# Stores of two blocks at a time, and q and k in four pieces, in an attention and expert kernel

## The chip, the cores and the metric

The kernel runs on one core of a Trainium2 chip. The core has a matrix engine (TensorE, PE in the profile; its weight loads are PEld), three engines for elementwise work (VectorE = DVE, ScalarE = ACT, GpSimd = POOL), a sequencer that here only issues transfers (SyncE = SP, "SPq"), and 16 DMA engines. The metric is the device time of one execution in microseconds (us), as a median of several runs. A profile shows one further execution.

## The reference

Attention with a sliding window of 128 and a linear bias, over 8 batches, 8 heads, 576 positions and 64 elements a head; its result x (4608 tokens of 512) goes through eight experts, all of them applied to all tokens and weighted by a matrix P that eight rounds of row and column normalisation make from the gate's logits.

```python
def _attn_ref(q, k, v):
    scores = scale * np.matmul(q, k.transpose(0, 1, 3, 2))
    rel = pos[:, None] - pos[None, :]
    bias = slopes[:, None, None] * (-np.abs(rel).astype(np.float32))[None, :, :]
    mask = (rel >= 0) & (rel < window)
    scores = np.where(mask, scores + bias[None], -1000000000.0)
    ...
    return np.matmul(attn, v).astype(np.float32)

def _moe_ref(x, w_gate, w1, w2):
    logits = x @ w_gate
    logits = logits - logits.max()
    P = np.exp(logits)
    for _ in range(8):
        P /= P.sum(1, keepdims=True) + 1e-09
        P /= P.sum(0, keepdims=True) + 1e-09
        P *= N / E
    out = np.zeros((N, D), dtype=np.float32)
    for e in range(E):
        h = np.maximum(x @ w1[e], 0.0)
        ye = h @ w2[e]
        out += P[:, e:e + 1] * ye
    return out.astype(np.float32)
```

## The kernel before

The program is written in the order in which each engine runs it (`tc.manual_schedule()`): an engine's queue is the order of the calls, and waits are put in where a tile's data or its buffer isn't there yet. SP issues nearly all transfers, so a transfer that must wait holds up those behind it.

**Attention stage (to about 284 us).** The main loop (L689) goes through 80 steps (b, kb, u): batch b, block kb of its five key blocks (four of 128 positions and a last one of 64), half u of the heads; at = 2 kb + u is the step within a batch. A step does the next step's scores (PE, L403) and exponentials (ACT, L426), its masks (DVE, L438), and its own values (L449: PE into a tile psN, then a reciprocal and a product on DVE into the tile xsb). When both halves of a block are there, `turn_x` (L496) turns it into xT: on PE for batches 0 to 2 and 7, with a transposing DMA (L519) for batches 3 to 6. It also puts the block on the list `kept`, from which `keep_x` stores it to the DRAM tensor xd (L494), three blocks later. Batch 0 occupies about 10 to 34 us; from batch 3 on (107 us) a batch takes 32 to 37 us.

**Filler.** PE's free time in these steps is filled with experts 0 and 1 (class Filler, L170), whose results need no P. A unit is four blocks of x and one expert: eight pieces of the first layer (`l1`, L109: four matmuls into psh, then a ReLU on ACT, L127) and four of the second (`l2`, L131: eight matmuls into psy, L137). Each l2 ends in `keep` (L545): DVE casts psy to a tile yo (L555), and a store to the DRAM tensor ysp is put on the list `stores`. `store(2)` ahead of each cast issues what is older than the last two (L541). The tag yo has YO = 6 tiles of 128 x 512 f16, so the cast of the sixth result after it waits until a result's store has landed. psy, psh, psN and some other PSUM tiles share the tag pmm, of four. Only the first four blocks of expert 0 go another way (y_first, L551). A batch has about eight l2.

**q and k.** Batch b + 2 is loaded at step (b, 3) for b = 1 to 5: `load_qk(b + 2)` (L766), one transfer of 1 MB each for q and k into two tiles (L271). They are cast to f16 by `cast_qk`, q on DVE (L287) and k on ACT (L289), two heads at a time: pieces 0 and 1 at steps (b, 8) and (b, 9), pieces 2 and 3 at (b + 1, 0) and (b + 1, 1). From batch 3 on `turn_qk` (at = 1, two transposing DMAs, L301), then `load_tail` (L260, "t") and `turn_tail` (at = 5, tT, L320) follow on SP. `load_v` (L374) follows every block.

**Afterwards.** The gate's logits are turned into P on DVE (L814 to L852) while the filler goes on, to about 326 us; then the main expert loop (L1104, experts 2 to 7, with a fast matrix product of seven products) reads xd two blocks at a time into xtok (L880), scales them (L888), turns them with transposing DMAs (L898) and adds the stored results of experts 0 and 1 (`load_y`, L1021). xs, xtok and s3 take buffers of the tag yo there, and t16 (the tails) takes one of the tag xsb (XSB = 12).

Of the kernel before, what the change touches and what calls it, by code (L numbers as in the profile page):

```python
# [9 lines left out]
FP16 = mybir.dt.float16  # L10
FP32 = mybir.dt.float32
# [3 lines left out]
def kernel(  # L15
# [10 lines left out]
    nc = tc.nc  # L26
# [137 lines left out]
            yield 0, a  # L164

    L1_US, L2_US = 0.87, 1.74
    XPE, YO, XSB = 3, 6, 12
    CAST_AT = ((0, 1, 2, 3), (1, 2, 3, 4))

    class Filler:  # L170
# [57 lines left out]
    sps = first_pool.enter_context(tc.tile_pool(name="sps", bufs=1, space=bass.MemoryType.PSUM))  # L228
    if True:
        mask = asb.tile([P, H, 2 * P], FP16, name="mask")  # L230
        rel = per.tile([P, HD], FP16, name="rel", tag="yo", bufs=YO)[:, 0 : 2 * P]

        def make_mask(ys):
            for y in ys:
# [27 lines left out]
                )  # L262
            tails[b] = t32

        def load_qk(b, parts=1):
            q32 = per.tile([P, H, RI * Dh], FP32, name=f"q32_{b}", tag="a8", bufs=8)
            k32 = per.tile([P, H, RI * Dh], FP32, name=f"k32_{b}", tag="a8", bufs=8)
            w = H // parts
            for n in range(parts):
                for t, src in ((q32, q), (k32, k)):  # L270
                    nc.sync.dma_start(  # L271
                        out=t[:, n * w : n * w + w],
                        in_=src[b, n * w : n * w + w, 0:SM, :].rearrange("h (p i) d -> p h (i d)", i=RI),
                    )
            raw[b] = (q32, k32)

        def cast_qk(b, j, which=(1, 0), pool=False):

# [36 lines left out]
                )  # L315

        def turn_tail(b):
            t16 = asb.tile([P, HD], FP16, name=f"t16_{b}", tag="xsb", bufs=XSB)
            nc.gpsimd.tensor_copy(out=t16, in_=tails.pop(b).rearrange("p h d -> p (h d)"))
            nc.sync.dma_start(out=QKT[b][2], in_=t16, transpose=True)  # L320

# [123 lines left out]
            )  # L445

        xsbs: dict = {}

        def values(b, kb, u):  # L449

            nk, _ = sizes(kb)
            if u == 0:
                xsbs[b, kb] = asb.tile([P, H, Dh], FP16, name=f"xsb_{b}_{kb}", tag="xsb", bufs=XSB)
            psN = aps.tile([P, GT], FP32, name=f"psN_{b}_{kb}_{u}", tag="pmm", bufs=4)
            if b == 0:
                spin(psN, 3)
            psN = psN[:, 0 : 4 * Dh + 4].rearrange("p (h d) -> p h d", h=4)
            ops = []
            for y in range(2):
                for hb in range(2):  # L460
                    hh = 2 * y + hb
                    if kb > 0:
                        ops.append((hh, pts[b, kb - 1, u][:, 2 * hb + y, P : P + nk], vs[b, kb - 1][:, 4 * u + hh, 0 : Dh + 1]))
                    ops.append((hh, pts[b, kb, u][0:nk, 2 * hb + y, 0:nk], vs[b, kb][0:nk, 4 * u + hh, 0 : Dh + 1]))
            if kb == NKB - 1:
                ops = ops[0::2] + ops[1::2]
            for i, (hh, lhsT, rhs) in enumerate(ops):
                nc.tensor.matmul(  # L468
                    out=psN[0:nk, hh, :],
                    lhsT=lhsT,  # L470
                    rhs=rhs,
                    start=(i == 0),
                    stop=(i == len(ops) - 1),
                )
            if kb > 0:
                pts.pop((b, kb - 1, u))
            rden = asb.tile([P, 4], FP32, name=f"rden_{b}_{kb}_{u}", tag="rden", bufs=2)
            nc.vector.reciprocal(out=rden[0:nk, :], in_=psN[0:nk, :, Dh])
            nc.vector.tensor_tensor(
                out=xsbs[b, kb][0:nk, 4 * u : 4 * u + 4, :],  # L480
                in0=psN[0:nk, :, 0:Dh],
                in1=rden[0:nk, :].unsqueeze(2).to_broadcast([nk, 4, Dh]),
                op=ALU.mult,
            )
# [5 lines left out]

        def keep_x(left=0):
            while len(kept) > left:
                blk, lo, nk, xsb = kept.pop(0)
                nc.sync.dma_start(out=xd[blk, lo : lo + nk, :], in_=xsb[0:nk].rearrange("p h d -> p (h d)"))  # L494

        def turn_x(b, kb):  # L496
            nk, _ = sizes(kb)
            blk = 4 * b + kb if kb < NKB - 1 else 4 * B + b // 2
            lo = 0 if kb < NKB - 1 else TL * (b % 2)
            xT, at = x_of(blk)  # L500
            to = xT[:, at, :, lo : lo + nk]
            xsb = xsbs.pop((b, kb))
            if by_pe(b):
                ps = aps.tile([P, NDT, P], FP16, name=f"psX_{b}_{kb}", tag="pmm", bufs=4)
                for j in range(NDT):
                    nc.tensor.matmul(
                        out=ps[:, j, 0:nk],
                        lhsT=xsb[0:nk, 2 * j : 2 * j + 2, :],
                        rhs=ident[0:nk, 0:nk],
                        is_transpose=True,  # L510
                        start=(j == 0),
                        stop=(j == NDT - 1),
                    )
                if b == 0:
                    nc.scalar.copy(out=to, in_=ps[:, :, 0:nk])
                else:
                    nc.vector.tensor_copy(out=to, in_=ps[:, :, 0:nk])  # L517
            else:
                nc.sync.dma_start(out=to, in_=xsb[0:nk].rearrange("p h d -> p (h d)"), transpose=True)  # L519
            kept.append((blk, lo, nk, xsb))  # L520
            keep_x(3)

        def gates(b0, b1):
            ps = aps.tile([P, b1 - b0, E], FP32, name=f"psG_{b0}", tag="pmm", bufs=4)
# [13 lines left out]
        def store(left=0):  # L538
            while len(stores) > left:
                e, blk, yo = stores.pop(0)  # L540
                nc.sync.dma_start(out=ysp[e, blk], in_=yo)  # L541

        first_y: list = []

        def keep(e, blk, ps):  # L545
            if blk < RI and e == 0:
                if not first_y:
                    first_y.append(per.tile([P, RI, HD], FP16, name="y_first", tag="a8", bufs=8))
                nc.vector.tensor_copy(out=first_y[0][:, blk, :], in_=ps)
                if blk == RI - 1:  # L550
                    nc.sync.dma_start(out=ysp[0, 0:RI].rearrange("m p d -> p m d"), in_=first_y[0])  # L551
                return
            store(2)
            yo = per.tile([P, HD], FP16, name=f"yo_{e}_{blk}", tag="yo", bufs=YO)
            nc.vector.tensor_copy(out=yo, in_=ps)  # L555
            stores.append((e, blk, yo))

        order = [(0, 0, 2), (0, 2, 2)]
        for b0 in range(RI, NBLK, 4):
# [92 lines left out]
        load_first()  # L652
        spin_alone(20)
        make_mask(range(4))
        load_qk(1, 2)
        load_v(NKB)
        load_tail(1)
        cast_v(0)
# [30 lines left out]
        for n, (b, kb, u) in enumerate(steps):  # L689
# [67 lines left out]
            if (b, at) == (1, 2):  # L757
                filler.hold = False
            if (b, at) == (0, 9):
                load_qk(2, 2)  # L760
            if (b, at) == (0, 7):
                homes(1)
            if (b, at) == (1, 3):
                homes(2)
            if 1 <= b < B - 2 and at == 3:
                load_qk(b + 2)  # L766
            if XPE <= b + 1 < B - 1 and at >= 8:
                cast_qk(b + 2, at - 8)
            if XPE <= b + 1 < B:
# [112 lines left out]
        def scale_x(n):  # L882
            if n >= N:
                return
            g, e = units[n]
            for m in range(2):
                blk = 2 * g + m
                nc.scalar.mul(out=xs[2 * (n % 2) + m], in_=xtok[m], mul=P_sb[:, blk, e : e + 1])  # L888
            if e == E - 1 and n + 1 < N:
                if g == groups[0]:  # L890
                    xtok[:] = [per.tile([P, HD], FP16, name=f"xtok_{i}", tag="yo", bufs=YO) for i in range(2)]
                load_x(units[n + 1][0])

        def turn_xs(n):
# [19 lines left out]
        def quads_w1(e):  # L914
# [5 lines left out]
            elif e == E - 1:  # L920
                t = per.tile([P, 2, 2, HF], FP16, name=f"s_{e}", tag="xT", bufs=4)
                q.update(s1=t[:, 0], s2=t[:, 1])
                q["s3"] = [per.tile([P, HF], FP16, name=f"s3_{k}", tag="yo", bufs=YO) for k in range(2)]
            else:
                q.update((f"s{i}", aux[:, i].rearrange("p f n -> p (f n)").rearrange("p (k f) -> p k f", k=2)) for i in (1, 2, 3))
            q["s4"] = q["a21"]
            SL[e] = q

            def one(to, a, b, op):
                if isinstance(q[to], list):  # L930
                    for k in range(2):
                        nc.vector.tensor_tensor(out=q[to][k], in0=q[a][:, k], in1=q[b][:, k], op=op)
                else:
                    nc.vector.tensor_tensor(out=q[to], in0=q[a], in1=q[b], op=op)

            one("s1", "a21", "a22", ALU.add)
            one("s3", "a11", "a21", ALU.subtract)
# [30 lines left out]
        def part(n, ps, w, x, start=False):  # L968

            q = SL[units[n][1]][w]  # L970
            q = q if isinstance(q, list) else [q[:, k] for k in range(2)]
            for j in range(NF2):
                for k in range(2):
                    nc.tensor.matmul(  # L974
                        out=ps[:, j, :],
                        lhsT=q[k][:, P * j : P * j + P],
                        rhs=xset[n % 2][:, x, P * k : P * k + P],
                        start=(start and j == 0 and k == 0),
                        stop=(k == 1),
# [119 lines left out]
        s5 = s5y[:, 0].rearrange("p (f t) -> p f t", f=NF2)  # L1099
        y = s5y[:, 1].bitcast(FP16).rearrange("p (m d) -> p m d", m=2)  # L1100
        turn_xs(1)
        xs[:] = [per.tile([P, HD], FP16, name=f"xs_{i}", tag="yo", bufs=YO) for i in range(2)] * 2
        late: tuple = ()
        for n in range(N):  # L1104
            g = units[n - 1][0]
# [103 lines left out]
```

## Time and profile before

| what | us |
|---|---|
| median of 3 runs (lowest, highest) | 1025.33 (1023.34, 1028.51) |
| the profiled execution | 1025.63 |
| its span in the profile | 1023.9 |
| PE busy / DVE / ACT / POOL | 1000.3 / 749.5 / 722.2 / 78.8 |
| ysp<-yo stores: 68 of 128 KB, issue to landing, median | 3.3 |
| xd<-xsb stores: 32 of 128 KB and 8 of 64 KB | 3.1 and 5.1 |
| q and k loads of 1 MB: 5 each | 7.8 and 10.1 |
| q and k pieces of 256 KB at the start: 4 each | 5.2 and 4.8 |
| s5y<-ysp loads of 256 KB: 36 | 3.0 |

The granted TensorE clock is 1.00 throughout. In a timeline a row has the start in us, the duration, the engine, the line, the operation and its tiles (out<-in), and in brackets the idle time ahead of it and what ended it. SPq rows are issues: their duration is the time for which SP was held. A row of waits has the total, the number and the longest.

### The profile page before, as it was taken

To read this page: it belongs to the slowest core of one execution; us is meant where nothing else is said; L and a number is where in the kernel's file an instruction comes from. 1 tells how busy PE (TensorE), PEld (TensorE's weight loads), DVE (VectorE), ACT (ScalarE), POOL (GpSimd) and SP (SyncE) were. 2 spreads that over 40 slices of the span, in tenths; PEclk is the share of its full clock that TensorE was granted. 3 is DMA by queue.
4 is the path that set the end of the run, shared out by engine and by line. 5 is a ranking of instruction groups with operands and counts; after the bars stand their busy time and mean duration, and the time that the engine had idled before them with its cause. 6 is when DMAs were issued, how large, how long until landed. Compare 5 with 4: busy or idle time off the path is not lost.

```text
span 1023.9 us, 27787 instructions
## 1 busy us (share of the span) xinstructions
PE 1000.3 (98%) x11487; PEld 801.6 (78%) x11487; DVE 749.5 (73%) x1594; ACT 722.2 (71%) x1240; POOL 78.8 (8%) x143
## 2 busy tenths in 40 slices
PE   7999999999999999999999999999999999999998
PEld 5645444444544698999999999999999999999997
DVE  5735665556578588877877877877887887787787
ACT  7646555555433457888888888888888888888885
POOL 1212033306110000000000000000000000000000
PEclk9999999999999999999999999999999999999999
DMA  9996689889999233343334334324334434333461
GB/s 244 219 271 170 143 221 220 191 196 180 221 192 177 69 72 80 71 81 94 74 64 100 76 66 94 73 64 94 77 65 98 81 71 81 86 82 65 98 115 47
DMA packets 264431, 122.46 MB, mean 120 GB/s; under 512 B 201968, under 2 KB 255728, under 8 KB 264304
## 3 DMA queue, kind: packets, MB, share of 16 engines
q1 hardware_dynamic: 249568, 102.68, 44.2%
q0 software_dynamic: 14304, 17.84, 10.5%
q8 instruction: 90, 1.47, 0.6%
q14 instruction: 37, 0.30, 0.1%
q10 hardware_dynamic: 432, 0.16, 0.1%
HBM read 78.30 MB, written 23.59 MB: 100 GB/s over the span
## 4 chain that ended last, share of the span: by engine, by line
PE 74%; DVE 3%; DMA 1%; ACT 1%; issue 0%; DVEq 0%; ACTq 0%; SPq 0%
PE psM L1011 30%; PE psB L974 13%; PE psA L974 9%; PE psC L974 9%; PE psy L137 5%; PE psh L115 5%; PE psh L953 2%; DVE acc L1055 1%; PE psN L468 1%; DMA acc<-xd 0%; DVE hs L1141 0%; PE psS L412 0%; DVE hs L991 0%; DVE hs L992 0%; DMA s5y<-ysp 0%
## 5 line engine op out<-in xcount | busy, mean ns | idle before, releaser
L1011 PEld LDWEIGHTS <-hs 128*128 128x128 f16 x2996 | 271.7, 98 | 22.4
L1011 PE MATMUL psM<-w2l,hs 128*128 128x256 f16 x1440 | 186.6, 273 | 0.0
L974 PEld LDWEIGHTS <-w1l 128*128 128x128 f16 x2720 | 173.2, 98 | 8.9 <-issue 3.0
L127 ACT ACTIVATE hT<-psh 128x512 f16<-128x512 f32 (+1 forms) x144 | 83.3, 586 | 100.9 <-PE psh L115 100.2
L987 ACT ACTIVATE hs<-hs 128x512 f16<-128x512 f16 x204 | 125.0, 630 | 34.3 <-DVE hs L1141 34.1
L1141 DVE TENSOR_TENSOR hs<-psB,s5y 128x512 f16<-128x512 f32 x102 | 70.4, 690 | 103.7 <-ACT xs L888 95.9
L115 PE MATMUL psh<-xT,w1t 128*128 128x512 f16 (+1 forms) x608 | 139.8, 368 | 3.2 <-DVE xT L517 2.4
L974 PEld LDWEIGHTS <-s 128*128 128x128 f16 x2040 | 135.3, 98 | 5.8
L888 ACT ACTIVATE xs<-xtok,L_sb 128x512 f16<-128x512 f16 x204 | 136.0, 720 | 0.6 <-DMA xset<-xs 0.6
L137 PE MATMUL psy<-w2t,hT 128*128 128x512 f16 x576 | 134.3, 379 | 0.0
L1011 PE MATMUL psM<-more,hs 128*128 128x256 f16 x864 | 129.0, 273 | 0.0
L974 PE MATMUL psA<-xset,w1l 128*128 128x128 f16 x1360 | 103.7, 219 | 0.0
L974 PE MATMUL psB<-xset,s 128*128 128x128 f16 x1360 | 103.7, 219 | 0.0
L137 PEld LDWEIGHTS <-hT 128*128 128x128 f16 x576 | 53.5, 98 | 60.9 <-issue 1.5
L555 DVE CAST yo<-psy 128x512 f16<-128x512 f32 x68 | 46.8, 690 | 72.1 <-PE psy L137 57.8
L115 PEld LDWEIGHTS <-w1t 128*128 128x128 f16 x608 | 54.7, 98 | 54.7 <-issue 7.0
L991 DVE TENSOR_TENSOR hs<-hs 128x1024 f16<-128x1024 f16 x107 | 74.0, 691 | 23.5 <-ACT hs L987 16.8
L430 ACT ACTIVATE pt<-psS 128x1024 f16<-128x1024 f32 (+2 forms) x80 | 67.7, 851 | 29.2 <-PE psS L412 22.7
L1135 ACT COPY psC<-psB 128x512 f32<-128x512 f32 x102 | 58.1, 570 | 36.5 <-PE psB L974 36.5
L1130 ACT COPY s5y<-psC 128x512 f32<-128x512 f32 x102 | 59.8, 586 | 25.5 <-PE psC L974 25.5
L443 DVE TENSOR_TENSOR pt<-pt,mask 128x1024 f16<-128x1024 f16 (+2 forms) x80 | 51.8, 647 | 32.8 <-ACT pt L430 32.7
L1055 DVE TENSOR_TENSOR acc<-acc,psM 128x256 f32<-128x256 f32 (+1 forms) x162 | 74.1, 503 | 2.1
(121 smaller groups left out, 1410.1 us busy)
## 6 DMA issues: line engine op xcount, KB each, us to landing
s5y<-ysp SPq DMA_DIRECT2D x36, 256.0 KB, 3.0
ysp<-yo SPq DMA_DIRECT2D x68, 128.0 KB, 3.3
v<-in_v_dram SPq DMA_DIRECT2D x32, 256.0 KB, 4.4
out_dram<-acc SPq DMA_DIRECT2D x31, 256.0 KB, 2.5
q<-in_q_dram SPq DMA_DIRECT2D x5, 1024.0 KB, 7.8
k<-in_k_dram SPq DMA_DIRECT2D x5, 1024.0 KB, 10.1
xtok<-xd SPq DMA_DIRECT2D x34, 128.0 KB, 2.3
w2t<-in_moe_w_dram POOLq DMA_DIRECT2D x4, 1024.0 KB, 10.9
```

Of the source, the lines that this page charges most:

```text
L115: nc.tensor.matmul(out=ps[:, 0:nt], lhsT=w1ts[e][:, dt, P * ft : P * ft + P], rhs=xT[:, at : at + nb, dt, :], start=(dt == 0), stop=(dt == ...
L127: nc.scalar.activation(out=st["hT"][:, ft, 0:nt], in_=ps[:, 0:nt], func=AF.Relu)
L137: nc.tensor.matmul(out=ps, lhsT=st["hT"][:, ft, P * ms : P * ms + P], rhs=w2ts[e][:, ft, :], start=(ft == 0), stop=(ft == NFT - 1),)
L430: nc.scalar.activation(out=pt[0:nk, :, 0 : nk + nn], in_=ps[0:nk, :, :, 0 : nk + nn].rearrange("p a y n -> p (a y) n"), func=AF.Exp, scale ...
L888: nc.scalar.mul(out=xs[2 * (n % 2) + m], in_=xtok[m], mul=P_sb[:, blk, e : e + 1])
L974: nc.tensor.matmul(out=ps[:, j, :], lhsT=q[k][:, P * j : P * j + P], rhs=xset[n % 2][:, x, P * k : P * k + P], start=(start and j == 0 and ...
L987: nc.scalar.activation(out=h[n][:, slot], in_=src, func=AF.Relu)
L991: nc.vector.tensor_tensor(out=t[:, 4:6], in0=t[:, 0:2], in1=t[:, 2:4], op=ALU.add)
L1011: nc.tensor.matmul(out=Ms[bk][:, half, :], lhsT=h[n][:, LEFT[m], f, :], rhs=W2L[e][RIGHT[m]][:, f, :], start=(e == 2 and f == 0 and half = ...
L1055: nc.vector.tensor_tensor(out=a, in0=a, in1=p2, op=op)
L1130: nc.scalar.copy(out=s5, in_=pc)
L1141: nc.vector.tensor_tensor(out=h[n][:, 3], in0=pb, in1=s5, op=ALU.add)
```

## The change

Results of experts 0 and 1 are kept in tiles of two blocks (YO = 3 tiles of twice the size), stored with one transfer of 256 KB: `store(1)` runs when a pair is full, ahead of putting it on the list. Blocks of x go into tiles of two (XSB = 6); `keep_x` stores two blocks at once, and a batch's fifth, short block alone; one entry stays on the list in place of three. `load_qk` takes a number of pieces and which of them to load: for batches 3 to 7 it is called at steps 3, 4, 5 and 6, each time for two heads of q and of k, 256 KB each. Batches 1 and 2 are loaded in halves at once, as before. The users of the two tags (rel, t16, xtok, xs, s3) take one of the larger tiles where they took one or two.

```diff
-    XPE, YO, XSB = 3, 6, 12
+    XPE, YO, XSB = 3, 3, 6
...
-        def load_qk(b, parts=1):
-            q32 = per.tile([P, H, RI * Dh], FP32, name=f"q32_{b}", tag="a8", bufs=8)
-            k32 = per.tile([P, H, RI * Dh], FP32, name=f"k32_{b}", tag="a8", bufs=8)
-            w = H // parts
-            for n in range(parts):
-                for t, src in ((q32, q), (k32, k)):
+        def load_qk(b, of, parts):
+            if b not in raw:
+                raw[b] = tuple(
+                    per.tile([P, H, RI * Dh], FP32, name=f"{c}32_{b}", tag="a8", bufs=8) for c in "qk"
+                )
+            w = H // of
+            for n in parts:
+                for t, src in zip(raw[b], (q, k)):
                     nc.sync.dma_start(
                         out=t[:, n * w : n * w + w],
                         in_=src[b, n * w : n * w + w, 0:SM, :].rearrange("h (p i) d -> p h (i d)", i=RI),
                     )
...
-            if u == 0:
-                xsbs[b, kb] = asb.tile([P, H, Dh], FP16, name=f"xsb_{b}_{kb}", tag="xsb", bufs=XSB)
+            if u == 0 and kb % 2 == 0:
+                pair = asb.tile([P, 2, H, Dh], FP16, name=f"xsb_{b}_{kb}", tag="xsb", bufs=XSB)
+                xsbs[b, kb], xsbs[b, kb + 1] = pair[:, 0], pair[:, 1]
+                pairs[b, kb] = pair
...
-                blk, lo, nk, xsb = kept.pop(0)
-                nc.sync.dma_start(out=xd[blk, lo : lo + nk, :], in_=xsb[0:nk].rearrange("p h d -> p (h d)"))
+                blk, lo, nk, n, pair = kept.pop(0)
+                nc.sync.dma_start(
+                    out=xd[blk : blk + n, lo : lo + nk, :].rearrange("m p d -> p m d"),
+                    in_=pair[0:nk, 0:n].rearrange("p m h d -> p m (h d)"),
+                )
...
-            kept.append((blk, lo, nk, xsb))
-            keep_x(3)
+            if kb % 2:
+                kept.append((blk - 1, lo, nk, 2, pairs.pop((b, kb - 1))))
+            elif kb == NKB - 1:
+                kept.append((blk, lo, nk, 1, pairs.pop((b, kb))))
+            keep_x(1)
...
-                nc.sync.dma_start(out=ysp[e, blk], in_=yo)
+                nc.sync.dma_start(out=ysp[e, blk : blk + 2].rearrange("m p d -> p m d"), in_=yo)
...
-            store(2)
-            yo = per.tile([P, HD], FP16, name=f"yo_{e}_{blk}", tag="yo", bufs=YO)
-            nc.vector.tensor_copy(out=yo, in_=ps)
-            stores.append((e, blk, yo))
+            if blk % 2 == 0:
+                yos.append(per.tile([P, 2, HD], FP16, name=f"yo_{e}_{blk}", tag="yo", bufs=YO))
+            yo = yos[-1]
+            nc.vector.tensor_copy(out=yo[:, blk % 2, :], in_=ps)
+            if blk % 2:
+                store(1)
+                stores.append((e, blk - 1, yo))
...
-            if 1 <= b < B - 2 and at == 3:
-                load_qk(b + 2)
+            if 1 <= b < B - 2 and 3 <= at < 3 + NDT:
+                load_qk(b + 2, NDT, (at - 3,))
```

More of the change, by code (lines that the diff above doesn't have):

```diff
@@ L230 @@
         mask = asb.tile([P, H, 2 * P], FP16, name="mask")
-        rel = per.tile([P, HD], FP16, name="rel", tag="yo", bufs=YO)[:, 0 : 2 * P]
+        rel = per.tile([P, 2, HD], FP16, name="rel", tag="yo", bufs=YO)[:, 0, 0 : 2 * P]
         def make_mask(ys):
@@ L274, in load_qk @@
                     )
-            raw[b] = (q32, k32)
         def cast_qk(b, j, which=(1, 0), pool=False):
@@ L317, in turn_tail @@
         def turn_tail(b):
-            t16 = asb.tile([P, HD], FP16, name=f"t16_{b}", tag="xsb", bufs=XSB)
+            t16 = asb.tile([P, 2, HD], FP16, name=f"t16_{b}", tag="xsb", bufs=XSB)[:, 0]
             nc.gpsimd.tensor_copy(out=t16, in_=tails.pop(b).rearrange("p h d -> p (h d)"))
@@ L447 @@
         xsbs: dict = {}
+        pairs: dict = {}
         def values(b, kb, u):
             nk, _ = sizes(kb)
-            if u == 0:
-                xsbs[b, kb] = asb.tile([P, H, Dh], FP16, name=f"xsb_{b}_{kb}", tag="xsb", bufs=XSB)
+            if u == 0 and kb % 2 == 0:
+                pair = asb.tile([P, 2, H, Dh], FP16, name=f"xsb_{b}_{kb}", tag="xsb", bufs=XSB)
+                xsbs[b, kb], xsbs[b, kb + 1] = pair[:, 0], pair[:, 1]
+                pairs[b, kb] = pair
             psN = aps.tile([P, GT], FP32, name=f"psN_{b}_{kb}_{u}", tag="pmm", bufs=4)
@@ L540, in store @@
                 e, blk, yo = stores.pop(0)
-                nc.sync.dma_start(out=ysp[e, blk], in_=yo)
+                nc.sync.dma_start(out=ysp[e, blk : blk + 2].rearrange("m p d -> p m d"), in_=yo)
         first_y: list = []
+        yos: list = []
         def keep(e, blk, ps):
@@ L654 @@
         make_mask(range(4))
-        load_qk(1, 2)
+        load_qk(1, 2, range(2))
         load_v(NKB)
@@ L759 @@
             if (b, at) == (0, 9):
-                load_qk(2, 2)
+                load_qk(2, 2, range(2))
             if (b, at) == (0, 7):
@@ L890, in scale_x @@
                 if g == groups[0]:
-                    xtok[:] = [per.tile([P, HD], FP16, name=f"xtok_{i}", tag="yo", bufs=YO) for i in range(2)]
+                    t = per.tile([P, 2, HD], FP16, name="xtok", tag="yo", bufs=YO)
+                    xtok[:] = [t[:, 0], t[:, 1]]
                 load_x(units[n + 1][0])
@@ L922, in quads_w1 @@
                 q.update(s1=t[:, 0], s2=t[:, 1])
-                q["s3"] = [per.tile([P, HF], FP16, name=f"s3_{k}", tag="yo", bufs=YO) for k in range(2)]
+                q["s3"] = per.tile([P, 2, HF], FP16, name="s3_e", tag="yo", bufs=YO)
             else:
@@ L929, in one @@
             def one(to, a, b, op):
[L930 to L934, printed above, removed]
+                nc.vector.tensor_tensor(out=q[to], in0=q[a], in1=q[b], op=op)
             one("s1", "a21", "a22", ALU.add)
@@ L970, in part @@
             q = SL[units[n][1]][w]
-            q = q if isinstance(q, list) else [q[:, k] for k in range(2)]
             for j in range(NF2):
@@ L975, in part @@
                         out=ps[:, j, :],
-                        lhsT=q[k][:, P * j : P * j + P],
+                        lhsT=q[:, k, P * j : P * j + P],
                         rhs=xset[n % 2][:, x, P * k : P * k + P],
@@ L1101 @@
         turn_xs(1)
-        xs[:] = [per.tile([P, HD], FP16, name=f"xs_{i}", tag="yo", bufs=YO) for i in range(2)] * 2
+        t = per.tile([P, 2, HD], FP16, name="xs", tag="yo", bufs=YO)
+        xs[:] = [t[:, 0], t[:, 1]] * 2
         late: tuple = ()
```

## The prediction, made before the change was run

> **What bounds the kernel now.** I read the page's busy row first, then stretches of the attention stage, then the waits of DVE on transfers, then SP's own order of issues.
>
> ```profile
> PE 1000.3 (98%) x11487; PEld 801.6 (78%) x11487; DVE 749.5 (73%) x1594; ACT 722.2 (71%) x1240; POOL 78.8 (8%) x143
> ```
>
> PE is idle for 23.6 us of 1023.9. The stretches (length, then busy us and count of PE, PEld, DVE, ACT, POOL, the clock, the DMA share, GB/s) show where:
>
> ```profile
> 80.00:118.00 38.00, 36.21 (x300) 18.38 (x299) 24.76 (x61) 21.89 (x36) 9.00 (x15) 1.00 0.66 158
> 118.00:153.00 35.00, 32.73 (x267) 15.71 (x267) 22.77 (x53) 18.90 (x31) 8.74 (x13) 1.00 0.80 195
> 153.00:187.00 34.00, 32.66 (x260) 15.91 (x257) 19.82 (x45) 17.69 (x29) 9.23 (x16) 1.00 0.94 210
> 187.00:221.00 34.00, 33.70 (x265) 16.29 (x264) 20.74 (x47) 18.73 (x31) 8.65 (x16) 1.00 0.90 204
> 221.00:250.00 29.00, 29.00 (x229) 14.08 (x229) 16.88 (x37) 13.85 (x22) 10.34 (x17) 1.00 0.98 175
> ```
>
> From 80 to 250, where the edited transfers lie, PE is idle 1.79 + 2.27 + 1.34 + 0.30 + 0 = 5.7 us. That is all that better transfers can give back there; what they can lose has no such bound. DVE's and ACT's waits (total, times, longest) that bear on the change:
>
> ```profile
> ACT c L289 <- DMA k<-in_k_dram: 15.5, 5, 7.3
> ...
> DVE yo L555 <- DMA ysp<-yo: 11.7, 5, 3.2
> ```
>
> So the cast of an expert's result already waits at times for an older store to free its buffer, and ACT's cast of k waits for the 1 MB load. SP's order of issues in batch 3 (start, duration):
>
> ```profile
> 118.64 1.22 SPq L519 DMA_TRANSPOSE xT<-xsb  x1
> 119.92 1.42 SPq L494 DMA_DIRECT2D xd<-xsb  x1
> 121.39 0.42 SPq L374 DMA_DIRECT2D v<-in_v_dram  x1
> 121.91 6.18 SPq L301 DMA_TRANSPOSE qk<-c  x2
> 128.15 0.64 SPq L260 DMA_DIRECT2D t<-in_q_dram  x1
> 128.84 0.62 SPq L260 DMA_DIRECT2D t<-in_k_dram  x1
> 129.50 1.10 SPq L541 DMA_DIRECT2D ysp<-yo  x2
> ```
>
> SP is nearly full: a pair of transposes holds it for 6.2 us, and a store that stands behind them in program order goes out that much later. It matters only if somebody waits for that store.
>
> **The change, part by part.** Number the 68 results that pass the yo tiles 0 to 67 in the order of their casts; pair p holds 2p and 2p+1.
>
> *Stores: fewer issues.* A batch has 8 results and 5 blocks of x. The change drops 4 ysp issues and 2 xd issues; between 128 and 220 us most of either take 0.57 to 0.62 us, so 6 x 0.6 = 3.6 us of SP less per batch. The packets and bytes stay, so the DMA engines (share 0.80 to 0.98 above) win nothing.
>
> *q and k: more issues.* Eight of 256 KB instead of two of 1 MB, 6 more. A 256 KB piece took 0.39 to 0.47 us at the kernel's start and ysp issues 0.6 in this stage; I take 0.55 to 0.6, so 3.5 us more of SP. The two nearly cancel. What is gained is backpressure: after the 1 MB pair two ysp issues took 2.92 us instead of 1.2. The pieces also land sooner (at the start 3.3 to 5.8 us against medians of 7.8 and 10.1 for 1 MB), and each is needed four or five steps after its issue. That ends ACT's 15.5 us of waits, most of which PE doesn't see.
>
> [...]
>
> *The yo tiles: when a buffer comes free.* This decides. Before: six tiles; the store of result n is written into the program at result n+3, and its buffer is wanted at n+6: three results of room. After: three tiles of two; the store of pair p is written when pair p+2 is full (result 2p+5), and its buffer is wanted by the next cast, 2p+6: one result of room, 1.7 to 4 us on PE. In it SP must reach the store and the store must land. In SP's order pair p stands where the store of result 2p+2 stood. Landing: the 256 KB ysp load has 3.0 us and the 128 KB ysp store 3.3 as medians; the pair lies between 2.8 and 5 (stores behind the q/k load took up to 9). I take 3.6, and 1.2 more right behind q/k pieces.
>
> Behind the waiting cast on DVE stand the masks, the reciprocals and products of the values, and evacuations. PE goes on until it wants a fourth PSUM tile of tag pmm or the next mask. At result 14:
>
> ```profile
> 125.85 0.69 DVE L555 CAST yo<-psy 128x512 f16<-128x512 f32 x1 [0.63 <-PE psy L137]
> ...
> 126.06 1.02 PE L115 MATMUL psh<-xT,w1t 128*128 128x512 f16 x4
> ...
> 126.92 0.41 PE L468 MATMUL psN<-v,pt 128*128 128x65 f16 x8
> ...
> 127.16 1.02 PE L115 MATMUL psh<-xT,w1t 128*128 128x512 f16 x4
> ```
>
> The fourth tile is wanted at 127.16 and the cast ends at 126.54: room of 0.6 us. The same count gives 1.1 at results 22 and 30.
>
> Costs on PE, place by place:
> - Result 14 wants pair 4, which stands at 129.50. The xd issue at 119.92 falls away (1.4): 128.1 + 3.6 = 131.7, wanted at 125.9. Wait 5.8, less 0.6: **+5.2**.
> - Result 18 wants pair 6. All is 6 us later by then, so SP meets the program again; up to pair 6 stand three x transposes (1.2 each), eight pieces (4.8), tT (2.0), pair 5, xd and two v (2.4). From 134 that is about 149, landed 152.8; wanted at 142.0 + 6.3 = 148.3. Wait 4.5, room 0.9: **+3.6**.
> - Batch 4, result 22 wants pair 8, which stood at 166.96. One ysp less (0.7), q0 and k0 for the whole loads (2.1 - 1.2 = 0.9), and SP no longer late (its pair of transposes went out at 154.63, with their casts ended at 151.2: 3.4): 162.0 + 4.8 = 166.8 against 163.9; 2.9 less 1.1. Result 24 wants pair 9 behind tT, whose own cast ends at 171.0: 171.0 + 2.0 + 0.1 + 3.6 to 4.8 against 173.9; wait 3.4 in the middle, room 2.0 (a wait of 2.07 there left no gap in PE before). 1.8 + 1.4 = **+3.2**.
> - Batch 5, result 30 wants pair 12, behind v (199.1), q0 and k0 (1.2): 200.3, or 1.8 sooner where SP's lateness (188.72 against 186.5) is gone; 199.4 + 4.8 = 204.2 against 199.2; 5.0 less 1.1: **+3.9**.
> - Batch 2, result 10: pair 2 behind tT, out near 102, wait 2, room 1: **+1.0**. Batch 6 has no q/k load: **+0.3**.
> - Gone: the gaps that such waits and the late k made before, 1.69 us (145.98), 1.34 (183.33) and 0.3: **-3.3**.
>
> Sum 5.2 + 3.6 + 3.2 + 3.9 + 1.0 + 0.3 - 3.3 = **+13.9 us**. Bounds: with a landing of 2.8 and 2 us of room everywhere 3.0 + 1.7 + 0.1 + 0.6 + 2.2 - 3.3 = +4.3 is left; with 5 us of landing the seven waits grow by 1.4 each, +23.7.
>
> [...]
>
> *Costed at nothing.* After 284 us SP waits for the casts and not the reverse: a store goes out 0.03 us after its cast and lands 4 to 7.3 us later, while its buffer is wanted five results on, 17 us. xsb: six pairs, four taken in a batch, stored one pair later; a batch of 33 us hides it, and without that cover one xT transpose would be some 3 us late, for a filler unit that runs a batch later. xs, xtok and s3 take one pair instead of two tiles. The final loop keeps its transfers.
>
> **Profile and median.** The profiled execution took 1025.63 us, 1.7 more than its span; the median is 1025.33. So 1025.3 + 13.9 = 1039.2 us.
>
> **The rivals.**
> 1. *PSUM covers it.* If the four pmm tiles are handed out as they come free and not in turn, PE has some 3 us at each place: 2.8 + 1.5 + 0.4 + 2.0 - 3.3 = +3.4, 1028.7. For it: the wait of 2.07 us without a gap. Against it: 1.63 us of wait at 182.0 left 1.34.
> 2. *SP is relieved* (the other side). If SP reaches each pair within the room, that is 5 us sooner than its place says, the waits end, and with k early all of the 5.7 us of idle PE comes back: 1025.6 - 5.7 = 1019.9. For it: SP's backpressure goes, in batch 3 by its rows q 2.25 for 0.6, xT 2.55 for 1.2, tT 3.08 for 1.2, together 4.9 us. Against it: the 6.2 us of transposes stay and stand before pair 4. It decides where a pair lands within 1 us after the end of the even result's matmuls. [...]
> 3. *Every pair waits.* Landings of 5 us and more under the loads, and the pairs I left out of batches 5 and 6: +23.7 + 6 = +30, 1055.
> That a half pair must wait for the other half I leave out: at the start casts ran at 4.65 us while later pieces of the same tile were still landing (7.98).
>
> **Numbers.** Forecast 0.65, rival 1 0.15, rival 2 0.13, rival 3 0.07. Half a per cent, 5.1 us, is about what the measurement tells from no change: 1020.2 to 1030.5. Rival 2 gives faster 0.11 and same 0.02 (it stands just at the bound, and the first 80 us, with 9.6 us of idle PE, could add to it); rival 1 same 0.14; the rest is slower, 0.73. The range 1022 to 1055 leaves most of rival 2 and the upper half of rival 3 outside; the forecast's own is 1030 to 1050.
>
> **What would show it.** DVE's wait for ysp<-yo at L555's successor rises from 11.7 to 30 us or more, longest 5 to 7, first near 126 us; PE's idle time between 80 and 250 rises from 5.7 to about 20; from 350 on all is shifted alike. ACT's wait for k falls under 4 us. I am wrong if the pair store behind the two transposes lands before 127, or if DVE waits and PE doesn't.

## The result, and the profile after

The changed kernel takes 1043.38 us (median of 4 runs, 1041.93 to 1043.73) against 1025.45 for the kernel before: a ratio of 1.0172 with a 95% interval of 1.0144 to 1.0199. The forecast was 1039.2, slower, in a range of 1022 to 1055. The span of the profiled execution grew from 1023.9 to 1041.9, by 18.0 us.

The busy row and the TensorE clock's row from the page of the changed kernel:

```profile
PE 1008.8 (97%) x11487; PEld 804.4 (77%) x11487; DVE 747.7 (72%) x1593; ACT 722.0 (69%) x1240; POOL 77.6 (7%) x143
...
PEclk9999899989999999999999999999999999999999
```

The count of matmuls is the same, yet PE is busy 8.5 us longer, and idle 33.1 us (1041.9 - 1008.8) in place of 23.6. Two slices show a granted clock below 0.9, where the page before had none. The stretches of the attention stage (columns as in the prediction):

```profile
80.00:118.00 38.00, 35.13 (x277) 17.41 (x276) 22.49 (x54) 18.15 (x30) 9.05 (x17) 0.91 0.67 157
118.00:153.00 35.00, 31.56 (x242) 14.92 (x241) 17.77 (x43) 18.30 (x29) 7.80 (x12) 0.95 0.80 175
153.00:187.00 34.00, 30.69 (x236) 14.25 (x234) 18.91 (x45) 16.09 (x27) 8.17 (x15) 0.95 0.94 204
187.00:221.00 34.00, 29.45 (x219) 13.87 (x218) 16.46 (x38) 15.70 (x24) 7.74 (x13) 0.91 0.81 168
221.00:250.00 29.00, 29.00 (x229) 14.22 (x228) 17.92 (x43) 17.08 (x27) 5.57 (x9) 0.99 0.59 147
```

PE's idle time here is 2.87 + 3.44 + 3.31 + 4.55 + 0 = 14.2 us, against 5.7; and the clock, 1.00 in all five before, is 0.91 to 0.99. Behind result 38 nothing more is lost: the end of result 39 (255.8 us) is 18.7 us late, that of result 63 the same, and the end of the kernel 18.0.

Waits of DVE on transfers between 60 and 350 us (total, times, longest), in the changed kernel:

```profile
DVE yo L567 <- DMA ysp<-yo: 19.0, 6, 5.8
```

The total is too small. SP's issues in batch 3, and then DVE and PE around result 14, show a wait that this row doesn't hold:

```profile
123.68 1.22 SPq L526 DMA_TRANSPOSE xT<-xsb  x1
124.95 1.28 SPq L375 DMA_DIRECT2D v<-in_v_dram  x1
126.33 5.12 SPq L302 DMA_TRANSPOSE qk<-c  x2
131.49 0.89 SPq L260 DMA_DIRECT2D t<-in_q_dram  x1
132.44 0.63 SPq L260 DMA_DIRECT2D t<-in_k_dram  x1
133.11 0.63 SPq L551 DMA_DIRECT2D ysp<-yo  x1
```

```profile
128.96 1.89 PE L137 MATMUL psy<-w2t,hT 128*128 128x512 f16 x8
...
132.80 1.02 PE L115 MATMUL psh<-xT,w1t 128*128 128x512 f16 x4 [0.44 <-ACT hT L127]
...
134.51 1.89 PE L137 MATMUL psy<-w2t,hT 128*128 128x512 f16 x8 [0.24 <-ACT hT L127]
...
136.42 0.69 DVE L567 CAST yo<-psy 128x512 f16<-128x512 f32 x1 [6.16 <-PE psy L137]
...
137.12 1.37 DVE L444 TENSOR_TENSOR pt<-pt,mask 128x1024 f16<-128x1024 f16 x1
137.16 0.19 PE L472 MATMUL psN<-v,pt 128*128 128x65 f16 x1 [0.77 <-DVE yo L567]
...
138.55 0.39 PE L472 MATMUL psN<-v,pt 128*128 128x65 f16 x7 [1.20 <-DVE pt L444]
```

The row names psy as what ended DVE's 6.16 us of idle time. But psy's matmuls ended at 130.85, and the store of pair 4, out at 133.11, landed 3.2 us later, at 136.3: that is what the cast waited for, 5.6 us. Where the engine named had long been done, look for the transfer. Result 30, in the same timeline further on, is plain:

```profile
210.08 1.03 PE L115 MATMUL psh<-xT,w1t 128*128 128x512 f16 x4
...
210.94 0.41 PE L472 MATMUL psN<-v,pt 128*128 128x65 f16 x8
...
211.19 1.02 PE L115 MATMUL psh<-xT,w1t 128*128 128x512 f16 x4
...
216.02 0.69 DVE L567 CAST yo<-psy 128x512 f16<-128x512 f32 x1 [5.77 <-DMA ysp<-yo]
...
216.62 0.55 DVE L444 TENSOR_TENSOR pt<-pt,mask 128x768 f16<-128x768 f16 x1
216.76 3.57 PE L137 MATMUL psy<-w2t,hT 128*128 128x512 f16 x8 [4.55 <-DVE yo L567]
```

PE does three more tiles of the tag pmm (psh, psN, psh) while the cast waits, and stands still at the fourth until the cast ends. And the eight matmuls that follow, at a granted clock of 0.5 from 214.68 us on, take 3.57 us; eight like them took 1.89 at 128.96 us, at 1.00.

### The profile page after: what moved, and what is told of

It reads as the page before. It is cut to its first block, busy times and chain, and to the rows that moved or that the text cites. A ratio compares the mean times of both kernels' runs of the same rounds, so it can differ in the third digit from the quotient of the medians.

```text
span 1041.9 us, 27716 instructions
## 1 busy us (share of the span) xinstructions
PE 1008.8 (97%) x11487; PEld 804.4 (77%) x11487; DVE 747.7 (72%) x1593; ACT 722.0 (69%) x1240; POOL 77.6 (7%) x143
## 3 DMA queue, kind: packets, MB, share of 16 engines
q0 software_dynamic: 14304, 17.84, 10.4%
## 4 chain that ended last, share of the span: by engine, by line
PE 86%; DMA 5%; DVE 4%; SPq 3%; issue 1%; ACT 1%; POOL 0%; DVEq 0%; POOLq 0%; ACTq 0%
PE psM L1021 30%; PE psB L984 13%; PE psy L137 11%; PE psh L115 10%; PE psA L984 8%; PE psC L984 8%; DMA ysp<-yo 2%; PE psh L964 2%; PE psN L472 1%; DMA q<-in_q_dram 1%; DMA v<-in_v_dram 1%; PE psS L413 1%; SPq L375 1%; DVE yo L567 1%; SPq L273 1%
## 5 line engine op out<-in xcount | busy, mean ns | idle before, releaser
L115 PE MATMUL psh<-xT,w1t 128*128 128x512 f16 (+1 forms) x608 | 143.1, 375 | 3.2 <-DVE xT L524 2.3
L137 PE MATMUL psy<-w2t,hT 128*128 128x512 f16 x576 | 137.2, 385 | 8.4 <-DVE yo L567 8.2
L984 PEld LDWEIGHTS <-s 128*128 128x128 f16 x1904 | 126.3, 98 | 5.4
L984 PE MATMUL psB<-xset,s 128*128 128x128 f16 x1224 | 93.3, 219 | 0.0
L1141 ACT COPY s5y<-psC 128x512 f32<-128x512 f32 x102 | 59.8, 586 | 25.6 <-PE psC L984 25.6
## 6 DMA issues: line engine op xcount, KB each, us to landing
w2t<-in_moe_w_dram POOLq DMA_DIRECT2D x4, 1024.0 KB, 10.3
```

The source lines that it names most:

```text
L115: nc.tensor.matmul(out=ps[:, 0:nt], lhsT=w1ts[e][:, dt, P * ft : P * ft + P], rhs=xT[:, at : at + nb, dt, :], start=(dt == 0), stop=(dt == ...
L137: nc.tensor.matmul(out=ps, lhsT=st["hT"][:, ft, P * ms : P * ms + P], rhs=w2ts[e][:, ft, :], start=(ft == 0), stop=(ft == NFT - 1),)
L984: nc.tensor.matmul(out=ps[:, j, :], lhsT=q[:, k, P * j : P * j + P], rhs=xset[n % 2][:, x, P * k : P * k + P], start=(start and j == 0 and ...
L1141: nc.scalar.copy(out=s5, in_=pc)
```

## The experiments

**Which part, and is it the room?** "Room" is the number of results between the place where a store is written into the program and the cast that wants its buffer: three in the kernel before, at most one in the changed one.

Two-block yo tiles alone. The kernel before gets `keep` and `store` of the changed one and YO = 3 pairs; the stores of x and the loads of q and k are as before.

> The kernel before with the two-block yo tiles and their stores alone; xd and q/k as before. Room theory (a pair's store is written one result before its buffer is wanted): 1035 to 1048 us, casts wait 15 us or more for ysp stores, the granted clock falls below 1.00 in the attention stage. Rival, SP held by the q/k pieces: about 1025 us, since there are none. Rival, pairs of x blocks: about 1025 us.

1052.42 us, ratio 1.0257 (1.023 to 1.0284): the slowdown is here, above the expected 1035 to 1048, and more of it than in the whole change. Casts wait 37.7 us for ysp stores, up to 10.4.

The changed kernel without them:

```diff
-    XPE, YO, XSB = 3, 3, 6
+    XPE, YO, XSB = 3, 6, 6
...
-            if blk % 2:
-                store(1)
-                stores.append((e, blk - 1, yo))
+            store(2)
+            yo = per.tile([P, HD], FP16, name=f"yo_{e}_{blk}", tag="yo", bufs=YO)
+            nc.vector.tensor_copy(out=yo, in_=ps)
+            stores.append((e, blk, yo))
```

> The changed kernel with single yo tiles and single ysp stores as before; x pairs and q/k pieces stay. Room theory: 1020 to 1027 us, no PE gap over 2 us after 80 us, granted clock 1.00. Rival, SP held by the q/k pieces, or pairs of x blocks: 1035 us or more.

1022.53 us, ratio 0.9962 (0.9941 to 0.9983): faster than both kernels. The x pairs and the pieces of q and k are not the harm. Casts still wait 3.4 us for stores. One gap of the 2 us kind remained, 1.83 us; it is ended by a transposing DMA of x (xT<-xsb), not by a cast.

The pair stored as soon as it is full:

```diff
             if blk % 2:
-                store(1)
                 stores.append((e, blk - 1, yo))
+                store()
```

> The changed kernel, with a pair's store written right behind the cast that fills it (five results of room in place of one); all else stays. Room theory: 1020 to 1029 us, casts wait under 3 us in all for ysp stores, clock 1.00. Rival, the 256 KB stores themselves land too late or hold the DMA engines: 1038 us or more. Rival, SP held by q/k pieces: 1038 us or more. What could spoil it: SP now waits for the cast and holds up what stands behind, up to 3 us a batch.

1022.95 us, ratio 0.997 (0.9952 to 0.9988). The tiles, the 256 KB stores and all else are those of the changed kernel; only the line that writes the store into the program has moved. The same two stretches as above, in this kernel:

```profile
118.00:153.00 35.00, 33.85 (x277) 16.70 (x276) 23.81 (x54) 20.79 (x33) 9.64 (x15) 1.00 0.98 208
153.00:187.00 34.00, 34.00 (x271) 16.63 (x269) 20.89 (x47) 19.19 (x31) 8.79 (x15) 1.00 0.92 209
```

PE does 271 matmuls between 153 and 187 us in place of 236, and the clock is 1.00. No row in which a cast waits for a ysp store is left.

The reverse test, in the kernel before: single tiles, single stores, but as little room.

```diff
-            store(2)
+            store(4)
             yo = per.tile([P, HD], FP16, name=f"yo_{e}_{blk}", tag="yo", bufs=YO)
```

> The kernel before with store(4) in place of store(2): single tiles and single stores, but each store written one result before its buffer is wanted, as in the changed kernel. Room theory: 1033 to 1055 us, as slow as the changed kernel or slower, because every result and not every second one can wait. If the pairing itself (256 KB transfers, two-block tiles) is the cause: 1025 to 1028 us.

1050.83 us, ratio 1.0242 (1.0208 to 1.0275). DVE's waits in it:

```profile
DVE yo L555 <- DMA ysp<-yo: 56.3, 14, 7.2
```

Nothing is paired here, no issue is added, and the loss is larger than the changed kernel's. So it is the room.

A middle value, with `store(1)` ahead of the even result's tile:

> The changed kernel with store(1) moved ahead of the even result's tile instead of behind the odd result's cast: a pair's store is written one result after the pair is full and its next-but-one result wants no buffer of it until three results later. Room of three results as in the kernel before, against one (1043.4 us) and five (1022.95). Room theory: 1021 to 1027 us, clock 1.00. If only a store straight behind its cast helps: above 1032.

1024.98 us, ratio 0.9986 (0.9965 to 1.0006), casts waiting 5.4 us in two places. The clock was not 1.00 throughout: one gap of 2.28 us is followed by 3.4 us of half clock. The expectation miscounts: pair p is written at result 2p + 4 and wanted at 2p + 6, so the room is two results. The ladder of pairs with pieces is 1.0172 for less than one, 0.9986 for two, 0.997 for five; the step lies between the first two.

**What the pieces of q and k do.** The changed kernel with whole loads, `load_qk(b + 2, 1, (0,))` at step 3:

> The changed kernel with q and k of batches 3 to 7 loaded whole at step 3, as before. If the pieces help (they take SP's backpressure and the late k away): 1047 to 1054 us, near the kernel with two-block yo tiles alone (1052.4), which differs from this one in the x pairs only. If the pieces burden SP with their six issues more: 1036 to 1041 us.

1053.89 us, ratio 1.0259 (1.0218 to 1.03), against 1.0172 with the pieces. Behind whole loads the pair stores land later still (pair 8 9.0 us after its issue and pair 12 9.5, against 4.8 and 5.6 with the pieces): casts wait 31.3 us, up to 9.8, against 19.0 and 5.8. The pieces saved the change some 9 us. That it equals the kernel with yo pairs alone (1.0257) says that the x pairs change nothing that these runs resolve.

The pieces alone, in the kernel before:

> The kernel before with the four pieces of q and k alone. If the pieces are the whole gain of the kernel without yo pairs (0.9962): 1020 to 1024 us, ACT's waits for k under 4 us, the gap of 1.3 us near 182 gone. If the x pairs bring it: 1025 to 1027.

1025.71 us, ratio 0.9984 (0.996 to 1.0007). ACT's wait for k falls from 15.5 to 3.5 us and the gap near 182 from 1.34 to 0.42 as expected, but a gain can't be told from none. The time is in the range given for the x pairs, yet the intervals of the two ratios (0.9984 and 0.9962) overlap, so it doesn't show that they bring the gain. With whole loads and pairs stored when full:

> The changed kernel with pairs stored when full and q and k whole at step 3: what the pairing of stores is worth without the pieces. By the prediction's account (3.6 us of SP less a batch, PE covered): 1024 to 1027 us, the late k and its gap near 144 still there. If SP's relief matters by itself: 1021 to 1023.

1024.26 us, ratio 0.9974 (0.9955 to 0.9994), with 10.3 us of waits for k left, and two gaps of PE over 1.5 us between 80 and 360 us, the larger 1.71. That is the upper of the two expectations by time. But neither gap is the one near 144: there ACT still waits 5.8 us for k, and PE stands still for no more than 0.3 us at a time. So the late k alone did not make the gap that the kernel before has there, where a cast also waits 2.9 us for a store. By ratio the interval overlaps those of 0.997 and 0.9984. Which part of the 0.3% comes from SP's relief and which from the early k stays open.

**Is the low clock a cost of its own?** PE's lost time in the changed kernel is idle time and slow time: its granted clock is 0.5 from 108.87, 139.59, 177.13 and 214.68 us on, for 6.83, 3.41, 3.41 and 6.83 us. To separate the two, four or eight waits were put into the main expert loop of the kernel before, where no edited transfer runs and the clock is 1.00:

```diff
+        held = lp.tile([P, HB], FP16, name="held")
...
                 pa = bank(n, "A")
+                if n in (20, 40, 60, 80):
+                    for _ in range(8):
+                        nc.gpsimd.tensor_copy(out=held, in_=h[n - 1][:, 2, 0:2, :].rearrange("p f t -> p (f t)"))
+                    nc.tensor.matmul(out=pa[:, 0, :], lhsT=held[:, 0:P], rhs=held[:, 0:P], start=True, stop=True)
                 part(n, pa, "a11", B11, True)
```

> The kernel before with four waits of PE put into the main expert loop, far from all transfers that the change touches: at units 20, 40, 60 and 80 one extra matmul reads a small tile that eight GpSimd copies have to write first, by estimate 4.5 to 6 us of wait each. Clock theory (a gap that long leaves TensorE at half its clock for some 3.4 or 6.8 us): granted clock 0.5 behind each gap, and the time grows by more than the idle time of PE does, by 1.5 to 3.4 us a gap. Rival (the low clock in the changed kernel has another cause): clock 1.00, and the growth equals the idle time, 18 to 24 us.

1057.67 us, ratio 1.0294 (1.0268 to 1.032). The first of the four, in the timeline and then in stretches around it:

```profile
471.61 4.57 POOL L1127 COPY held<-hs 128x256 f16<-128x256 f16 x8 [151.29 <-ACT hs L988]
...
476.23 0.29 PE L1128 MATMUL psA<-held 128*128 128x128 f16 x1 [5.34 <-POOL held L1127]
```

```profile
400.00:470.00 70.00, 70.00 (x951) 66.14 (x949) 55.69 (x116) 58.00 (x102) 0.00 (x0) 1.00 0.33 70
470.00:483.00 13.00, 7.66 (x67) 6.59 (x66) 3.30 (x7) 4.60 (x9) 4.13 (x8) 0.74 0.29 78
```

A clock of 0.74 over 13 us is half the clock for 6.8 us (13 x 0.26 / 0.5). All four gaps (5.03 to 5.34 us) are followed by a stretch of half clock, two of 6.8 us and two of 3.4. (This execution had a fifth, of 3.4 us, at 110 us, which the sum below takes in.)

> The same with eight waits of half the copies (four), by estimate 2 to 3 us each: about the same idle time in shorter pieces. Clock theory: at most one or two stretches of half clock, and a growth that is close to the added idle time, 16 to 24 us. Rival: the same growth per us of idle time as with four long waits.

1071.17 us, ratio 1.0436 (1.037 to 1.0502): a miss. The gaps came out at 3.18 to 3.49 us, since four copies fewer made them only 1.85 us shorter (5.03 less 3.18, 5.34 less 3.49), and six of the eight were followed by half clock. The rival came out: the span grew by 1.6 us for each us of added idle time here, and by 1.5 with the four long waits.

> The same eight waits with one GpSimd copy each; four copies gave gaps of 3.2 to 3.5 us and eight 5.0 to 5.3, so 0.46 us a copy, and one copy should give 1.8 to 2.1 us. Clock theory: no half clock behind them, and the time grows by the added idle time, 14 to 17 us. Rival: half clock behind some of them too, and 18 us or more.

1038.33 us, ratio 1.0113 (1.009 to 1.0136): added idle time of 11.0 us, a span longer by 12.9, and no half clock behind these gaps. They were shorter than expected (three of 1.69 us and five of 1.38), and so the time grew by less than 14 us.

One sum comes within 2 us for these kernels but one, with idle time from PE's merged intervals and the granted clock from the profile's record; the slow share is half of PE's busy time at half clock, by estimate from the 3.57 us of the eight matmuls there against 1.89:

| kernel | span over before | idle over before | PE busy at half clock, halved | sum |
|---|---|---|---|---|
| the change | 18.0 | 9.5 | 8.4 | 17.9 |
| yo pairs alone | 24.7 | 15.8 | 8.0 | 23.8 |
| the change with whole loads | 27.1 | 15.7 | 10.5 | 26.2 |
| the kernel before with store(4) | 22.7 | 13.0 | 6.4 | 19.5 |
| four waits of 5 us | 31.1 | 20.6 | 10.7 | 31.3 |
| eight waits of 3.3 us | 40.4 | 25.6 | 13.6 | 39.2 |
| eight waits of 1.4 to 1.7 us | 12.9 | 11.0 | 0 | 11.0 |

What makes up the 3.2 us that the sum lacks with store(4) is not known.

**Beyond both kernels.** Single tiles with `store(1)`, four results of room:

> The changed kernel with single yo tiles and single stores as in the run without yo pairs (1022.53), and store(1) in place of store(2): four results of room in place of three. Room theory: the 3.4 us in which casts still waited there go, 1019 to 1023 us. If three results of room are enough: the same as there within 1 us.

1023.73 us, ratio 0.9962 (0.9944 to 0.9981). The cast's waits for stores are gone but for 0.5 us, and the ratio is that of the run without yo pairs: three results are enough there. In the profiled execution (1026.09, the slowest of ten) PE waited 3.33 us for a transposing DMA of x and then had 3.4 us of half clock: what is left there is a late transpose, not a late store. Both, and the pair stored when full, beat the kernel before by 0.3 to 0.4%.

## Why the prediction was right, and where its sum was not

**What bounds it, and the mechanism.** Right. The change's harm is that a pair's store is written one result ahead of the cast that wants its buffer, behind SP's transposes. Moving one line takes it away, and giving the kernel before the same lack of room brings it there.

**The places.** The end of each result's matmuls in both traces gives how late PE is at it; the differences are the price of a place. The last two columns split it as in the sum above.

| place | wait, predicted | wait, measured | price on PE, predicted | measured | of it idle time | of it half clock |
|---|---|---|---|---|---|---|
| result 10 | 2 | 2.8 | +1.0 | +4.2 | +1.5 | 2.8 |
| result 14 | 5.8 | 5.6 | +5.2 | +4.5 | +2.5 | 1.5 |
| result 18, with the gap near 144 gone | 4.5 | 1.4 | +1.9 | -1.3 | -1.1 | 0 |
| results 22 and 24, with the gap near 182 gone | 2.9 and 3.4 | 3.9 and none | +1.9 | +2.9 | +1.3 | 1.7 |
| result 30, with the gap near 217 gone | 5.0 | 5.8 | +3.6 | +6.4 | +4.2 | 2.4 |
| result 38 | not given | 2.2 | +0.3 | +1.2 | +1.0 | 0 |

The first late place before these (+0.8 near result 0) and -0.7 at the end make up the 18.0.

**The step that failed is the sum's size.** Every price was reckoned as idle time of PE, 13.9 us. Measured are 9.5 us of idle time and 8.4 us of work at half clock. The second term was missing: the page before shows a clock of 1.00 wherever it looks, and the prediction let PE resume at full speed behind a wait of 5 us. The term is not one execution's accident: the four executions of the changed kernel have a mean clock of 0.990 or 0.991, and the 61 of the kernel before that ran beside the experiments 0.992 to 1.00. The idle time was 4.4 us too large and the missing term 8.4, so the two errors cancel in part: the forecast's nearness (1039.2 against 1043.4) is luck to that extent.

The idle time was too large at two places, results 14 and 18 (PSUM room, below, has the first), and the second is linked to the missing term. At result 18 the prediction put pair 6 out at 149 and landed at 152.8; it went out at 149.27 and landed at 152.8. What was wrong is when it was wanted: PE was 9.5 us late by then and not 6.3, so the wait was 1.4 and not 4.5. Pair 9 likewise landed at 183.1, and result 24, 12.6 us late, wanted it at 186.5. Being later than reckoned, the program met these two transfers with 1.4 us of waiting and none.

**PSUM room.** Right at result 30, where the rows show PE stop at the fourth pmm tile behind psy, and at 10, 22 and 38, where the wait less the idle time it made (at result 22, 3.88 less 2.66) is 1.2 to 1.3 us, against the predicted 1.0 to 1.1. Wrong at result 14: the prediction took the psh of 127.16 for the tile that needs the buffer, with 0.6 us of room. In the changed kernel that psh (132.80) waits for ACT's ReLU and not for the cast, the psy of result 15 (134.51) starts before the cast too, and PE stops at the next psN (137.16). In the kernel before, that psN is this row:

```profile
130.30 0.41 PE L468 MATMUL psN<-v,pt 128*128 128x65 f16 x8
```

It starts 3.8 us behind the end of the cast at 126.54. So a wait of 5.6 us made 2.5 us of idle time and not the reckoned 5.2. The rival by which PSUM covers the waits had 2.8 us for this place and was near the measured 2.5; it falls in the whole, with +3.4 us against 9.5 of idle time and 18.0 in all.

**SP's relief.** The rival on the other side fell at its own point of decision: pair 4 lands at 136.3, 5.5 us after the end of result 14's matmuls, not within 1. What speaks for it is seen only once the stores are written in time: 0.997.

**The pieces of q and k.** The direction was right (ACT's wait for k falls from 15.5 to 1.2 us in the changed kernel), but its weight in the change was underrated: with whole loads the change costs 9 us more, by stores that land later behind them. The prediction listed that backpressure and then put 1.2 us on some landings; the whole loads cost casts 12 us more of waiting.

**What would show it.** DVE's row was to read 30 us or more and reads 19.0. One wait is put down to psy, but with its 6.16 us the row would read 25.2: the waits were fewer and shorter than reckoned. The waits read from store landings are 2.8 + 5.6 + 1.4 + 3.9 + 5.8 + 2.2 = 21.7. PE's idle time was to be about 20 us between 80 and 250 and is 14.2.

## What to carry to other kernels

Merging two transfers that free buffers moves the store later in the program and halves the number of buffers; count, in units of the producer, how long before its next use each buffer's store is written, and put beside it what the issuing queue does in that time and how long a landing takes. Write such a store right behind the instruction that fills its tile: the same pairing then went from 1.7% slower to 0.3% faster. With two results of room the harm was gone already (0.9986). Where waits stop the matrix engine, read the granted clock behind them too, and add the slow work to the price: here it was 8.4 us of the 18.0, behind gaps that made 9.5.

## What the runs showed of the hardware

TensorE's granted clock fell to half behind gaps of PE, for 3.4 or 6.8 us, once (whole loads) for 10.2: behind four of four gaps of 5.0 to 5.3 us, six of eight of 3.2 to 3.5, none of eight that GpSimd's single copy made (up to 1.69). In the changed kernel it did so four times, 20.5 us in all: behind gaps of 4.55 and 2.66 us, but also behind one of 1.57 and behind four of 0.24 to 1.20 that began within 5 us. So it was not the longest gap alone that decided here.

The traces show more of when it happened. The shorter half-clock stretches in the changed kernel's clock record last 3.413 us, and within a trace the stretches start whole multiples of that apart (in the changed kernel at 108.87, 139.59, 177.13 and 214.68 us: 9, 11 and 11 times). Cut into windows of 3.413 us that end where the stretches start, the changed kernel's trace has PE, by its merged intervals, idle for 47%, 58%, 78% and 72% of the window just ahead of the four; of its windows between 60 us and the last 12 with the clock at 1.00 and no half clock behind them, the idlest had 48%. Eight traces have such stretches ahead of their last 12 us: the changed kernel, yo pairs alone, whole loads, store(4), two results of room, the four long waits, the eight of 3.3 us, and single tiles with store(1) (mean clocks 0.985 to 0.998). Counted in the same way over all eight, PE was idle for 58% to 100% of the window just ahead of 27 of the 29 stretches, and for at most 56% of the windows without half clock behind them. The gaps of 0.77 and 1.20 us ahead of 139.59 lie in one window and make up its 58%; the gap of 3.18 us in the run with eight waits that had no half clock behind it lies across a border, with 39% and 55%. The other two stretches, at 108.87 us in the changed kernel and at 112.89 with store(4), follow windows of 47% and 45%; what set them off is not known. This is a count in these traces: windows idle for 58% had half clock behind them as well as wholly idle ones, and what governs the clock is not shown.
